# Handing a head pair's row maxima to the score matmuls: a transpose on TensorE against a block transpose on VectorE with the order made by the DRAM loads

## The chip, the cores and the metric

The kernel runs on one core of one Trainium2 chip. The metric is the device time of one execution in microseconds (us). Three executions of the kernel before took 2587.34, 2584.07 and 2585.78 us; the median is 2585.78 us. The engines are named as in the profile: PE is TensorE's matrix unit (PEld is its weight loader), DVE is VectorE, ACT is ScalarE, POOL is GpSimd, SP is SyncE, and SPq or ACTq is the instruction stream of SP or ACT where it issues a DMA (a transfer).

## The reference, cut to what matters

```python
x  = A_x                                   # 1 x 2048 x 576
xn = layernorm(x)
# A: attention with 32 heads of 18, no mask
q, k, v = split(xn @ wqkv)                 # per head 2048 x 18
p  = softmax(q @ k.T * 18 ** -0.5)         # per head 2048 x 2048
s  = concat_heads(p @ v) @ wo
# B: gated feed-forward, 4608 wide
h  = gelu_tanh(xn @ w_gate) * (xn @ w_up)
g  = silu(h @ w_down)
out = x + s * g
```

The softmax subtracts each row's maximum before the exponential. That maximum, one number for each of 2048 queries and each head, is what the change is about.

## The kernel before, in words

**Precision.** The inputs are float32. Before a matmul each operand is split into two float16 numbers, a high and a low part, and the products of the parts are summed.

**Stages.** A short first stage (about 200 us) normalises x, computes the first heads' projections and the row maxima of head pair 0. Then one long loop runs over the 16 head pairs (`for p in range(NPAIR)`, line 1685) with 64 steps each. Everything else, the remaining projections, the feed-forward matmuls (L492 for gate and up, L752 for down) and the output projection, is cut into small pieces and placed between those steps. The order of every engine's instructions is fixed when the program is built: a planner (`make_plan`, `Deferred`, `subtick`) decides with a table of assumed costs which piece follows which, and each engine then works through its own list in that order, waiting on semaphores where it must.

**One step** `i` of pair `p` has these parts:

- The *score pass* (`qk2`, L1395): two matmuls on PE, one per head, make a 128 x 512 block of transposed scores in a buffer `s2`. ACT turns it into exponentials (L1401, or L1403 and L1404 where the two heads need different scales). There is one buffer `s2`, so the next score pass waits until these exponentials are finished.
- The *max pass* (`qk1`, L1343): two matmuls on PE make a block of untransposed scores of pair p+1 (in steps 60 to 63 of pair p+2) in a buffer `s1`. DVE reduces it to row maxima (L1346, `PM`). There is one buffer `s1` as well, so the next max pass waits for that row max.
- Filler pieces on PE, and every few steps a *burst* (L1420) that multiplies the saved exponentials with the values, after which DVE adds the burst's PSUM result to a running sum (L1428, `osb`).

**How the maximum gets into the score pass.** In the score pass the keys' tile KT has 56 rows per head: 54 rows of split keys and two rows holding a constant 2^15. The queries' tile QT has 54 rows of split queries and two rows that hold minus the row maximum times 2^-15, as a high and a low part, for each of 2048 queries. So the matmul subtracts the maximum by itself. But the maxima come out of DVE with the queries on the 128 partitions, and the two rows of QT need the queries along a row. That turn is the handover, made once per pair in three pieces (`max_end`, line 1350), called from the loop for the next pair: `a` at the end of step 59, `b` at the end of step 60, `c` in step 62.

- `a` (DVE): the last reduction `rmx` (L1356) and the high and low parts `rmc` (L1358, L1359), 128 partitions x 64 float16: column = 32 * head + 16 * part + query tile.
- `b`: PE turns `rmc` to 64 x 128 in the PSUM buffer `md_t` (L1365), which bursts and down pieces use too. ACT copies it to SBUF (`rms`, L1367) and stores it in DRAM (`md`, L1369): 64 partitions of 256 bytes.
- `c`: ACT issues two loads, one per head (L1373). Each reads 32 of the 64 DRAM rows, which lie one behind another, as two runs of 4096 bytes, and writes them to the two rows of QT.

The first score pass of the new pair, which is one step after step 63, needs these rows. The handovers are numbered here by the pair that they serve: handover 0 is for pair 0 and lies ahead of the loop (there `b` and `c` stand elsewhere among the pieces), handovers 1 to 15 lie at steps 59 to 62 of pair 0 to 14.

The names in the profile: `s` is the score buffer, `P` the exponentials, `mc` is called `rmc`, `ms` is `rms`. L460 (`touch`) is a tiny DVE read that sets the order of two writers of a PSUM buffer. VT<-VS (L1335) is the load of a pair's values on SP's queue; rd, oc, sd and obr (L1456 to L1471) are small transfers of the softmax sums.

Of the kernel before, what the change touches and what calls it, by code (L numbers as in the profile page):

```python
# [13 lines left out]
F16 = mybir.dt.float16  # L14
I32 = mybir.dt.int32
AF = mybir.ActivationFunctionType
# [4 lines left out]
P = 128  # L21
NT = S // P
# [72 lines left out]
def kernel(ctx: ExitStack, tc: tile.TileContext, x, wqkv, wo, w_gate, w_up, w_down, out):  # L95
    nc = tc.nc
# [4 lines left out]
    sm = ctx.enter_context(tc.tile_pool(name="sm", bufs=3))  # L101
    wp = ctx.enter_context(tc.tile_pool(name="wp", bufs=2))
    ap = ctx.enter_context(tc.tile_pool(name="ap", bufs=2))
    dp = ctx.enter_context(tc.tile_pool(name="dp", bufs=1, space=DRAM))
# [89 lines left out]
    ident = cp.tile([P, P], F16, tag="ident", name="ident")  # L194
# [1123 lines left out]
    QT, KT, VT, PM = {}, {}, {}, {}  # L1318
# [31 lines left out]
    def max_end(p):  # L1350

        st = {}

        def a():
            st["mx"] = sm.tile([P, 2, NT], F32, tag="rmx", name=f"rmx{p}", bufs=2)
            nc.vector.tensor_reduce(st["mx"], PM[p], op=ALU.max, axis=AX.X, negate=True)  # L1356
            st["mc"] = sm.tile([P, 2, 2, NT], F16, tag="rmc", name=f"rmc{p}", bufs=2)
            nc.vector.tensor_scalar(st["mc"][:, :, 0, :], st["mx"], 2.0 ** -15, None, op0=ALU.mult)  # L1358
            nc.vector.scalar_tensor_tensor(  # L1359
                st["mc"][:, :, 1, :], st["mx"], 2.0 ** -15, st["mc"][:, :, 0, :], op0=ALU.mult, op1=ALU.subtract  # L1360
            )

        def b():
            mt = MTile("md", [P, 2048], F16, 0)
            nc.tensor.transpose(mt.t[0:64, 0:P], st["mc"].rearrange("p a b c -> p (a b c)"), ident)  # L1365
            st["ms"] = sm.tile([64, P], F16, tag="rms", name=f"rms{p}", bufs=2)
            nc.scalar.activation(st["ms"], mt.t[0:64, 0:P], AF.Copy)  # L1367
            st["md"] = dp.tile([64, P], F16, tag="md", name=f"md{p}", bufs=2)
            nc.scalar.dma_start(st["md"], st["ms"])  # L1369

        def c():
            for h in range(2):
                nc.scalar.dma_start(  # L1373
                    QT[p][54 + 64 * h:56 + 64 * h, :],
                    st["md"][32 * h:32 * h + 32, :].rearrange("(a t) c -> a (t c)", a=2),
                )
            mdone[p] = 1

        return a, b, c
# [138 lines left out]
    while isinstance(pj1[0], Rest) or pj1[0][0] is None:  # L1518
        f = pj1.pop(0)
# [346 lines left out]
```

## Time and profile before

| | before |
|---|---|
| three runs | 2584.07 to 2587.34 us, median 2585.78 us |
| span of the profiled execution, first to last instruction | 2583.5 us |
| PE busy | 2503.6 us (97%) |
| DVE busy | 1894.5 us (73%) |
| ACT busy | 1660.4 us (64%) |
| POOL busy | 1536.8 us (59%) |
| mean granted TensorE clock | 0.997 |

The profile gives the profiled execution's span, 2583.5 us, and no device time of its own; the median of the three runs is 2.3 us above it, and that is taken as what lies around the span. Times in the views are from the span's start. In a timeline a row reads: start, duration, engine, line, operation, output<-inputs, shapes, how many alike were merged, and in brackets how long the engine had been idle before it and what released it. Matmuls overlap: a pair of 512-column matmuls takes 0.22 us of PE's time, though each is shown with 0.38 to 0.40 us. A row x2 at L1395 or L1343 is one pass (two heads).

### The profile page before, as it was taken

What the parts mean: (1) busy time and instruction counts of PE and PEld (TensorE: products, weight loads), DVE (VectorE), ACT (ScalarE), POOL (GpSimd) and SP (SyncE); (2) the same over time, 40 slices, a digit from 0 to 9 for tenths busy, and PEclk for the clock granted to TensorE, in tenths of its full rate; (3) what the DMA queues carried; (4) which work ended last, traced back from release to release, by engine and by line L of the source; (5) the groups of instructions that cost most, each with busy time, mean ns of one, the idle gap of its engine ahead of it and who ended that gap; (6) DMA issues with size and microseconds to landing.
All of it is one profiled execution on the core that took longest, in us unless ns stands there. A gap on an engine that the chain in (4) does not pass through costs nothing.

```text
span 2583.5 us, 60864 instructions
## 1 busy us (share of the span) xinstructions
PE 2503.6 (97%) x25816; PEld 1316.9 (51%) x25816; DVE 1894.5 (73%) x2595; ACT 1660.4 (64%) x2082; POOL 1536.8 (59%) x1545
## 2 busy tenths in 40 slices
PE   7899999999999999999999999999999999999998
PEld 6554445444544454445445545454544555455555
DVE  7677768777787778777777777776777777777644
ACT  6126666766677666766666666667666666766664
POOL 4346664576357564667576675848576676757513
PEclk9999999999999999999999999999999999999999
DMA  4430121201130112111110111201111111010124
GB/s 154 132 94 21 19 55 43 75 14 29 52 87 16 22 45 63 32 38 47 19 52 16 33 40 29 56 11 37 29 34 29 38 22 45 9 49 12 37 63 139
DMA packets 134635, 118.69 MB, mean 46 GB/s; under 512 B 59691, under 2 KB 113713, under 8 KB 134362
## 3 DMA queue, kind: packets, MB, share of 16 engines
q1 hardware_dynamic: 130089, 106.39, 15.8%
q0 software_dynamic: 1568, 5.37, 0.6%
q8 instruction: 202, 3.31, 0.5%
q10 hardware_dynamic: 2704, 3.03, 0.4%
q14 instruction: 72, 0.58, 0.1%
HBM read 84.89 MB, written 29.61 MB: 44 GB/s over the span
## 4 chain that ended last, share of the span: by engine, by line
PE 82%; DVE 7%; POOL 3%; ACT 3%; issue 2%; DMA 2%; SPq 0%; ACTq 0%; POOLq 0%; DVEq 0%
PE mb_t L492 16%; PE md_t L752 15%; PE ma_t L492 15%; PE md_t L1420 9%; PE s L1395 8%; PE s L1343 8%; PE ma_t L1420 6%; DVE PM L1346 3%; ACT P L1401 1%; PE md_t L931 1%; DVE osb L1428 1%; DMA QT<-QD 1%; POOL raw_c L356 1%; PE pv_t L511 1%; PE mb_t L931 1%
## 5 line engine op out<-in xcount | busy, mean ns | idle before, releaser
L1346 DVE TENSOR_REDUCE PM<-s 128x2 f32<-128x1024 f32 x1024 | 1251.0, 1224 | 335.5 <-PE s L1343 327.6
L1401 ACT ACTIVATE P<-s,etab 128x1024 f32<-128x1024 f32 x896 | 995.6, 1112 | 590.2 <-PE s L1395 579.4
L492 PE MATMUL ma_t<-XHT,whi_c 64*128 64x512 f16 x1440 | 542.0, 376 | 4.3 <-DVE osb L1428 2.2
L492 PE MATMUL mb_t<-XHT,whi_c 64*128 64x512 f16 x1440 | 541.7, 376 | 2.3 <-DVE touch L460 1.5
L492 PE MATMUL ma_t<-XHT,wlo_c 64*128 64x512 f16 x1296 | 487.4, 376 | 0.0
L492 PE MATMUL ma_t<-XL,whi_c 64*128 64x512 f16 x1152 | 433.2, 376 | 0.0
L492 PE MATMUL mb_t<-XHT,wlo_c 64*128 64x512 f16 x1152 | 433.2, 376 | 0.0
L492 PE MATMUL mb_t<-XL,whi_c 64*128 64x512 f16 x1152 | 433.0, 376 | 0.0
L1395 PE MATMUL s<-QT,KT 56*128 56x512 f16 x2048 | 404.4, 380 | 6.6 <-ACT P L1401 2.6
L1343 PE MATMUL s<-KT,QT 54*128 54x512 f16 x2048 | 398.3, 378 | 12.0 <-DVE PM L1346 9.7
L492 PEld LDWEIGHTS <-whi_c 64*128 64x128 f16 x5184 | 273.9, 94 | 241.0 <-issue 19.3
L752 PE MATMUL md_t<-dhi_c,hhi 64*128 64x288 f16 x2304 | 341.3, 283 | 4.8 <-DVE touch L460 2.1
L752 PE MATMUL md_t<-dhi_c,hlo 64*128 64x288 f16 x2304 | 341.0, 282 | 0.0
L752 PE MATMUL md_t<-dlo_c,hhi 64*128 64x288 f16 x2304 | 340.5, 282 | 0.0
L752 PEld LDWEIGHTS <-hhi 64*128 64x128 f16 x4608 | 246.7, 94 | 140.4 <-issue 16.8
L715 POOL TENSOR_TENSOR hlo<-gv,hhi 128x512 f16<-128x512 f32 x144 | 167.3, 1162 | 215.0 <-ACT hhi L708 210.7
L693 POOL TENSOR_SCALAR tw<-tw 128x512 f32<-128x512 f32 x144 | 90.7, 630 | 341.2 <-ACT tw L686 340.9
L1420 PE MATMUL md_t<-P,VT 128*32 128x512 f32 x2472 | 291.9, 596 | 0.5 <-ACT P L1401 0.5
L1395 PEld LDWEIGHTS <-KT 56*128 56x128 f16 x2048 | 123.5, 94 | 244.2 <-issue 156.4
L680 POOL TENSOR_TENSOR tw<-gs 128x512 f32<-128x512 f32 x144 | 151.0, 1049 | 125.2 <-ACT gs L657 125.1
L772 DVE SCALAR_TENSOR_TENSOR y<-md_t,c_c,y 128x576 f32<-128x576 f32 x272 | 219.5, 807 | 8.2 <-PE md_t L752 8.2
L492 PEld LDWEIGHTS <-wlo_c 64*128 64x128 f16 x2592 | 138.0, 94 | 118.9
(270 smaller groups left out, 4061.5 us busy)
## 6 DMA issues: line engine op xcount, KB each, us to landing
draw_c<-in_B_w_down SPq DMA_DIRECT2D x18, 576.0 KB
raw_c<-in_B_w_gate SPq DMA_DIRECT2D x18, 512.0 KB
raw_c<-in_B_w_up SPq DMA_DIRECT2D x18, 512.0 KB
obr<-rd SPq DMA_DIRECT2D x30, 256.0 KB
KT<-KD SPq DMA_DIRECT2D x32, 224.0 KB
QT<-QD SPq DMA_DIRECT2D x32, 216.0 KB
VS<-vst POOLq DMA_DIRECT2D x16, 304.0 KB, 2.6
VT<-VS SPq DMA_DIRECT2D x16, 304.0 KB
```

The lines of the kernel that those rows point to most:

```text
L492: nc.tensor.matmul(o, lw, xx, start=self.stage == 0 and self.k == 0, stop=self.stage == 1 and self.k == self.slots - 1, skip_group_check=True,
L680: gp.tensor_tensor(st["t"], st["g"], st["g"], op=ALU.mult)
L693: gp.tensor_scalar(st["t"], st["t"], 1.0, 1.0, op0=ALU.mult, op1=ALU.add)
L715: gp.tensor_tensor(hs.lo[:, ft], st["v"], hs.hi[:, ft], op=ALU.subtract)
L752: nc.tensor.matmul(self.t.t[:, hf, 0:288], a[r, ft, sl], b[r, ft, 288 * hf:288 * hf + 288], start=self.stage == 0 and k == 0, stop=self.st ...
L772: nc.vector.scalar_tensor_tensor(yy, y, w.c, yy, op0=ALU.mult, op1=ALU.add)
L931: nc.tensor.matmul(o, a, b, start=self.stage == 0 and self.k == 0, stop=self.stage == 1 and self.k == len(terms) - 1, skip_group_check=True,)
L1343: nc.tensor.matmul(s1[:, h], QT[p][r, P * qt:P * qt + P], KT[p][r, 512 * kb:512 * kb + 512], start=True, stop=True)
L1346: nc.vector.tensor_reduce(PM[p][:, :, qt, kb:kb + 1], s1, op=ALU.max, axis=AX.X)
L1395: nc.tensor.matmul(s2[:, h], KT[p][r, P * kt:P * kt + P], QT[p][r, 512 * qb:512 * qb + 512], start=True, stop=True)
L1401: nc.scalar.activation(pt, s2, AF.Exp, scale=ETAB[j0])
L1420: nc.tensor.matmul(t.t[qd:qd + 32, :], VT[p][:, c0:c0 + 32], pt[:, h], start=kt == k0, stop=kt == k1, skip_group_check=True,)
```

## The change

`b` no longer uses PE, PSUM or an ACT copy. DVE transposes `rmc` in blocks of 32 x 32 to a tile `mt` (still named `rms`) of 128 partitions x 64, and ACT stores that to DRAM as 128 rows of 128 bytes. After the block transpose, row 32 * b + 16 * part + tile of `mt` holds at column 32 * head + j the value for query 128 * tile + 32 * b + j. So a head's row of QT lies in DRAM in 64 pieces of 32 values (64 bytes), and `c`'s two loads pick these up in order by their access pattern. `a` and the places of `a`, `b` and `c` in the loop are as before.

```diff
         def b():
-            mt = MTile("md", [P, 2048], F16, 0)
-            nc.tensor.transpose(mt.t[0:64, 0:P], st["mc"].rearrange("p a b c -> p (a b c)"), ident)
-            st["ms"] = sm.tile([64, P], F16, tag="rms", name=f"rms{p}", bufs=2)
-            nc.scalar.activation(st["ms"], mt.t[0:64, 0:P], AF.Copy)
-            st["md"] = dp.tile([64, P], F16, tag="md", name=f"md{p}", bufs=2)
-            nc.scalar.dma_start(st["md"], st["ms"])
+            st["mt"] = sm.tile([P, 64], F16, tag="rms", name=f"rms{p}", bufs=2)
+            nc.vector.transpose(st["mt"], st["mc"].rearrange("p a b c -> p (a b c)"))
+            st["md"] = dp.tile([P, 64], F16, tag="md", name=f"md{p}", bufs=2)
+            nc.scalar.dma_start(st["md"], st["mt"])
 
         def c():
+            md = st["md"]
             for h in range(2):
                 nc.scalar.dma_start(
-                    QT[p][54 + 64 * h:56 + 64 * h, :],
-                    st["md"][32 * h:32 * h + 32, :].rearrange("(a t) c -> a (t c)", a=2),
+                    QT[p][54 + 64 * h:56 + 64 * h, :].rearrange("a (t b j) -> a t b j", t=NT, b=4),
+                    bass.AP(
+                        tensor=md.tensor, offset=md.offset + 32 * h,
+                        ap=[[NT * 64, 2], [64, NT], [2 * NT * 64, 4], [1, 32]],
+                    ),
                 )
             mdone[p] = 1
```

The rest of the program keeps its order on all engines; only the numbers in names differ, and lines below the change are numbered two higher. Three places show what moves, all at handover 9.

On DVE, before: `s_9_63` is the last max pass for pair 9, `s_10_0` and `s_10_1` are the max passes of steps 60 and 61.

```order
L1346 TENSOR_REDUCE PM_19121<-s_9_63_21563 128x2
L1428 TENSOR_TENSOR osb_1_20724<-md_t,osb_1_20724 128x512
L1356 TENSOR_REDUCE rmx_21589<-PM_19121 128x32
L1358 TENSOR_SCALAR rmc_21591<-rmx_21589 128x2x16
L1359 SCALAR_TENSOR_TENSOR rmc_21591<-rmx_21589,rmc_21591 128x2x16
L1346 TENSOR_REDUCE PM_21302<-s_10_0_21599 128x2
L1346 TENSOR_REDUCE PM_21302<-s_10_1_21633 128x2
```

And with the change:

```order
L1356 TENSOR_REDUCE rmx_21571<-PM_19105 128x32
L1358 TENSOR_SCALAR rmc_21573<-rmx_21571 128x2x16
L1359 SCALAR_TENSOR_TENSOR rmc_21573<-rmx_21571,rmc_21573 128x2x16
L1346 TENSOR_REDUCE PM_21284<-s_10_0_21581 128x2
L1365 STREAM_TRANSPOSE rms_21604<-rmc_21573 128x64
L1346 TENSOR_REDUCE PM_21284<-s_10_1_21613 128x2
```

The new transpose stands behind the row max of step 60, not right behind `rmc`, because `b` is recorded at the end of step 60. In handovers 1, 4 and 12 the sum of a burst (`osb`) stands ahead of it as well, in handover 11 a reduction of weights (L262); in handovers 0 and 15 it follows `rmc` directly.

On ACT, before (`P_2_14` to `P_3_15` are the exponentials of steps 60 to 63 of pair 8, `P_0_0` the first of pair 9):

```order
L1401 ACTIVATE P_2_14_21597<-s_8_2_14_21594,etab_5383 128x1024
L1367 ACTIVATE rms_21624<-md_t 64x128
L1369 DMA md_21626<-rms_21624 64x128
L1401 ACTIVATE P_3_14_21631<-s_8_3_14_21628,etab_5383 128x1024
L1401 ACTIVATE P_2_15_21661<-s_8_2_15_21658,etab_5383 128x1024
L1373 DMA QT_19115<-md_21626 2x2048 x2
L686 ACTIVATE tw_0_1_21603<-tw_0_1_21603 128x512
L1401 ACTIVATE P_3_15_21707<-s_8_3_15_21704,etab_5383 128x1024
```

And with the change:

```order
L1403 ACTIVATE P_2_14_21579<-s_8_2_14_21576,etab_5379 128x1024
L1367 DMA md_21606<-rms_21604 128x64
L1403 ACTIVATE P_3_14_21611<-s_8_3_14_21608,etab_5379 128x1024
L1403 ACTIVATE P_2_15_21641<-s_8_2_15_21638,etab_5379 128x1024
L1372 DMA QT_19099<-md_21606 2x64x32 x2
L686 ACTIVATE tw_0_1_21585<-tw_0_1_21585 128x512
L1403 ACTIVATE P_3_15_21687<-s_8_3_15_21684,etab_5379 128x1024
```

The store stays where it was, between the exponentials of steps 60 and 61; the copy ahead of it is gone.

On PE, before:

```order
L492 MATMUL mb_t<-XHT,wlo_c_19573 128x512
L1365 LDWEIGHTS rmc_21591
L1365 MATMUL md_t<-ident,rmc_21591 64x128
L1395 LDWEIGHTS KT_16878
L1395 MATMUL s_8_3_14_21628<-QT_16877,KT_16878 128x512
L1395 LDWEIGHTS KT_16878
L1395 MATMUL s_8_3_14_21628<-QT_16877,KT_16878 128x512
L1343 LDWEIGHTS QT_21296
L1343 MATMUL s_10_1_21633<-KT_21297,QT_21296 128x512
```

With the change the two L1365 rows are not there, and the score pass of step 61 follows the filler directly:

```order
L492 MATMUL mb_t<-XHT,wlo_c_19555 128x512
L1397 LDWEIGHTS KT_16864
L1397 MATMUL s_8_3_14_21608<-QT_16863,KT_16864 128x512
L1397 LDWEIGHTS KT_16864
L1397 MATMUL s_8_3_14_21608<-QT_16863,KT_16864 128x512
L1343 LDWEIGHTS QT_21278
L1343 MATMUL s_10_1_21613<-KT_21279,QT_21278 128x512
```

So PE loses its wait for `rmc` ahead of the score pass of step 61, and its max pass of step 61 comes next as before.

## The prediction

> **What bounds the kernel now.** I read the page first, then the groups by line of PE. One row of each kind:
>
> ```profile
> span 2583.5 us, 60864 instructions
> L1343 PE MATMUL s<-KT,QT 54*128 54x512 f16 x2048 | 398.3, 378 | 12.0 <-DVE PM L1346 9.7 <-DMA QT<-QD 0.9 <-DVE touch L460 0.2
> L1365 PE MATMUL md_t<-ident,rmc 128*64 128x128 f16 x16 | 3.8, 238 | 4.4 <-DVE osb L1428 2.4 <-DVE rmc L1359 1.9
> L1365 PEld LDWEIGHTS <-rmc 128*64 128x64 f16 x16 | 1.7, 106 | 10.3 <-DVE rmc L1359 6.1 <-issue 1.7 <-DVE PM L1346 1.7
> ```
>
> PE is the full engine (97% in the table ahead), so whatever delays PE for good is time. The sixteen turns (L1365) look costly: PE idles 4.4 us before them, its weight loader 10.3 us, mostly for DVE. But the max pass L1343 also waits for DVE's row max, 9.7 us in all, so I followed the single handovers in the timeline, on PE, DVE and ACT together. Handover 9, the common kind:
>
> ```profile
> 1530.27 1.22 DVE L1346 TENSOR_REDUCE PM<-s 128x2 f32<-128x1024 f32 x1
> 1530.40 0.24 PE L1365 MATMUL md_t<-ident,rmc 128*64 128x128 f16 x1 [0.17 <-DVE rmc L1359]
> 1530.58 0.39 PE L1395 MATMUL s<-QT,KT 56*128 56x512 f16 x2
> 1530.98 0.46 ACTq L1369 DMA_DIRECT2D md<-rms  x1
> 1531.49 1.11 ACT L1401 ACTIVATE P<-s,etab 128x1024 f32<-128x1024 f32 x1 [0.54 <-PE s L1395]
> 1531.54 0.39 PE L1343 MATMUL s<-KT,QT 54*128 54x512 f16 x2 [0.57 <-DVE PM L1346]
> 1531.97 1.23 DVE L1346 TENSOR_REDUCE PM<-s 128x2 f32<-128x1024 f32 x1 [0.48 <-PE s L1343]
> 1533.13 0.40 PE L1395 MATMUL s<-QT,KT 56*128 56x512 f16 x2
> 1533.57 1.11 ACT L1401 ACTIVATE P<-s,etab 128x1024 f32<-128x1024 f32 x1 [0.96 <-PE s L1395]
> ```
>
> The reader is to see that PE turns, makes its score pass (step 61), and then stands 0.57 us at the max pass until the row max of step 60 ends (1530.27 + 1.22 = 1531.49). DVE, not PE, sets the time of that max pass. A PE that reaches it earlier waits longer.
>
> **The change part by part.** *PE's turn goes.* In ten handovers (2, 3, 5 to 10, 13, 14) the max pass behind the turn waits for the row max as in handover 9; there the removal alone gives nothing. In the others it can give something, below.
>
> *DVE gets a transpose.* For its duration I take the line through a DVE operation on 32 columns, 0.19 us (L1359), and the block transposes that the kernel has already, on 512:
>
> ```profile
> 2432.81 0.19 DVE L1359 SCALAR_TENSOR_TENSOR rmc<-rmx,rmc 128x32 f16<-128x32 f32 x1
> L1443 DVE STREAM_TRANSPOSE obr<-osb 128x512 f32<-128x512 f32 x2 | 1.4, 712 | 0.1
> L1358 DVE TENSOR_SCALAR rmc<-rmx 128x32 f16<-128x32 f32 x16 | 6.5, 408 | 0.6
> L1467 SPq DMA_DIRECT2D rd<-oc x30: 319/336/417, 296.0 to 2454.9; - x30
> ```
>
> (0.712 - 0.19) / 480 = 1.09 ns a column, so 64 columns take 0.22 us. Lower bound 0.19. Upper bound: L1358 has 32 columns too and yet a mean of 0.41 us, so some small DVE operations are stretched; if the transpose is one of those it takes 0.4 us and more. I take 0.22. It stands between two row maxima, where DVE idles 0.48 us (1531.97): covered. Were that cover gone it would cost 0.22 x 16 = 3.5 us.
>
> *The store now waits for DVE.* It is still ahead of the exponentials of step 61 on ACT, but the transpose it waits for stands behind the row max of step 60. From the end of that row max: transpose 0.22, release 0.05 (as from 1531.49 to 1531.54), issue 0.34 (L1467 also moves 128 pieces of 64 bytes), next ACT instruction 0.05 (1530.98 + 0.46 to 1531.49): 0.66 us. In handover 9 the exponentials start at 1531.49 + 0.66 = 1532.15 instead of 1531.49, end 1.11 later, and release the next score pass at 1533.31 instead of 1533.13: **0.18 us lost**, because a new wait takes the place of the old one. Handover 14 is the other end of the ten:
>
> ```profile
> 2284.53 1.22 DVE L1346 TENSOR_REDUCE PM<-s 128x2 f32<-128x1024 f32 x1
> 2287.61 0.39 PE L1395 MATMUL s<-QT,KT 56*128 56x512 f16 x2 [0.24 <-ACT P L1401]
> ```
>
> 2285.75 + 0.66 + 1.11 + 0.05 = 2287.57, level with 2287.61: there ACT's copy and store were in the way already. Five of the ten (3, 5, 8, 9, 10) read like handover 9, two lose about 0.05, three (2, 7, 14) nothing: 5 x 0.18 + 0.1 = **1.0 us lost**. Bounds: 0.5 with a 0.19 us transpose and a shorter issue, 4 with 0.41 us and a longer one.
>
> *Handovers behind a burst (1, 4, 12).* The turn shares `md_t` with the burst and waits for DVE to add its result. Handover 12, then handover 15, where the transpose follows `rmc` directly, then 11:
>
> ```profile
> 1981.79 0.69 DVE L1428 TENSOR_TENSOR osb<-md_t,osb 128x512 f32<-128x512 f32 x1 [0.75 <-PE md_t L1420]
> 1982.53 0.22 PE L1365 MATMUL md_t<-ident,rmc 128*64 128x128 f16 x1 [0.81 <-DVE osb L1428]
> 1983.60 1.12 ACT L1401 ACTIVATE P<-s,etab 128x1024 f32<-128x1024 f32 x1 [0.54 <-PE s L1343]
> 1984.76 0.39 PE L1395 MATMUL s<-QT,KT 56*128 56x512 f16 x2
> 2433.35 0.24 PE L1365 MATMUL md_t<-ident,rmc 128*64 128x128 f16 x1
> 2434.45 1.11 ACT L1401 ACTIVATE P<-s,etab 128x1024 f32<-128x1024 f32 x1 [0.54 <-PE s L1395]
> 2435.61 0.39 PE L1395 MATMUL s<-QT,KT 56*128 56x512 f16 x2
> 1832.00 0.67 DVE L262 TENSOR_REDUCE m_c<-raw_c 128x1 f32<-128x512 f32 x1
> 1833.09 0.69 ACT L1403 ACTIVATE P<-s,etab 128x512 f32<-128x512 f32 x1 [0.54 <-PE s L1343]
> ```
>
> In 12 PE could go on about 1.0 us sooner (0.81 of wait, and the turn), but the transpose stands behind `osb` too: 1982.48 + 0.66 = 1983.14 for the exponentials instead of 1983.60. PE gains 0.46, in handover 1 as much: **0.9 gained**. In 15 `rmc` is ready at 2432.81 + 0.19 = 2433.00 and the store is out by 2433.00 + 0.22 + 0.05 + 0.34 = 2433.61, so the exponentials wait for PE alone: the score pass takes the turn's place at 2433.35, exponentials 0.44 later (1533.13 to 1533.57), 2433.79 instead of 2434.45: **0.65 gained**. In 11 the transpose stands behind a weight reduction that ends at 1832.67: 1832.67 + 0.66 = 1833.33 instead of 1833.09, **0.25 lost**.
>
> *The loads.* Before, a head's two rows are two runs of 4096 bytes; now 128 pieces of 64 bytes. What that costs is not in the trace; the nearest rows are two other transfers (issue, then windows with PE, PEld, DVE, ACT, POOL, clock, share of the 16 DMA engines, GB/s), and the tightest handover, 13:
>
> ```profile
> 1514.10 0.56 SPq L1335 DMA_DIRECT2D VT<-VS  x1
> 1515.00:1515.40 0.40, 0.40 (x6) 0.19 (x4) 0.40 (x1) 0.40 (x1) 0.40 (x1) 1.00 0.00 0
> 1515.60:1516.90 1.30, 1.30 (x18) 0.80 (x16) 0.79 (x2) 0.68 (x2) 1.30 (x2) 1.00 1.17 200
> 585.00:587.00 2.00, 2.00 (x22) 0.93 (x20) 1.78 (x3) 0.80 (x2) 0.00 (x0) 1.00 0.26 99
> 1176.80:1177.10 0.30, 0.30 (x6) 0.16 (x4) 0.30 (x1) 0.30 (x1) 0.30 (x1) 1.00 0.28 28
> 2139.36 0.54 ACTq L1373 DMA_DIRECT2D QT<-md  x2
> 2142.54 0.40 PE L1395 MATMUL s<-QT,KT 56*128 56x512 f16 x2
> ```
>
> VT<-VS moves 2048 pieces of 152 bytes in rows of 16; it is issued in 0.56 us, moves nothing for 1.3 us, then all 16 engines at 200 GB/s: 12.5 GB/s an engine, 12 ns a piece. The window at 585 is obr<-rd, whose source has 4 rows: share 0.26, four engines. So I expect two engines for a source and target with 2 rows at the outside, 64 pieces each: issue 0.56 each, data from 1.3 us on, 64 x 12 ns = 0.8 us. First head 2.1 us after the first issue, second 2.7 (own engines) to 2.9 (the same two). Handover 13 leaves 2142.54 - 2139.36 = 3.18 us: hidden, barely. The upper bound is oc<-sd, 128 pieces of 64 bytes on 16 engines within 0.3 us: up to 37 ns a piece, 128 x 37 ns + 1.3 = 6 us. I stay near 12 ns, since that is a long stream and the other is mostly start. The Trainium skill (DMA: Bandwidth & Descriptors, section "Why a DMA increments its semaphore by 16 and not by 1") says that a transfer runs on the largest number of engines up to 16 that divides the slowest dimension of both sides, and on the lowest-numbered ones: by it both loads share two engines and the second lands at 2.9 us.
>
> Handover 4 is short of that already, since its store meets VT<-VS:
>
> ```profile
> 786.74 0.54 ACTq L1373 DMA_DIRECT2D QT<-md  x2
> 787.33 0.69 ACT L1403 ACTIVATE P<-s,etab 128x512 f32<-128x512 f32 x1 [1.25 <-DMA QT<-md]
> 788.64 0.39 PE L1395 MATMUL s<-QT,KT 56*128 56x512 f16 x2 [1.04 <-ACT P L1404]
> ```
>
> ACT stands at the loads until the store has landed, and PE waits for ACT. Two issues of 0.56 instead of 0.54 together put the exponentials 0.6 us later, and the second head's rows land at 786.74 + 2.9 = 789.64, 1.0 us after the pass that needs them: **1.0 lost** (0.3 if the store lands 0.5 us earlier and the heads don't share engines; 1.5 if a piece takes 16 ns).
>
> *Handover 0* runs while the first weights load:
>
> ```profile
> 185.60 0.24 PE L1365 MATMUL md_t<-ident,rmc 128*64 128x128 f16 x1 [0.87 <-DVE rmc L1359]
> 190.50:194.90 4.40, 4.38 (x41) 2.05 (x39) 1.23 (x2) 0.00 (x0) 3.94 (x5) 1.00 0.77 221
> ```
>
> PE gains up to 1.2 us at the turn (0.87, the turn and its neighbours), and the loads, at 64 pieces an engine among transfers that hold 77% of the engines, may come up to 3 us late. I take zero.
>
> Sum: gained 0.9 + 0.65 = 1.55; lost 1.0 + 0.25 + 1.0 = 2.25. The profiled execution becomes 2583.5 + 0.7 = 2584.2; with the 2.3 us by which the runs' median of 2585.8 lies above the span, **2586.5 us**: no change that can be measured. A measurement of this kernel tells about 0.2%, 5.2 us, from no change.
>
> **The rivals.** *The whole turn comes out (faster).* PE gets its own 16 x 0.18 us (1530.40 to 1530.58) and between 4.4 and 10.3 us of wait: 7.3 to 13.2, about 10 us, 2576 us. For it: PE is the engine that is full. Against it: behind ten of the turns stands a wait for the same DVE, and the store's new place. It needs the store not to hold ACT.
>
> *The loads come late (slower).* One mechanism, at the first score pass of each new pair: 64-byte pieces on two engines. It decides from 3.2 us after the issue, that is from about 15 ns a piece; at 25 ns, half way to the upper bound, the second head lands at 1.3 + 128 x 0.025 = 4.5 us, and handover 13 loses 1.3 us. Eleven of fifteen handovers leave under 4 us between those two rows, about 1 us lost each: 11 us, **2597 us**. For it: the pieces are small and few engines carry them. Against it: VT<-VS at 12 ns.
>
> *The transpose is stretched (slower).* Like L1358, 0.41 us: each of the ten loses 0.19 more, and so does the burst's gain: 2.5 us, 2589 us; to pass 5.2 us it would have to take twice that. Against it: the transposes of L1443 show 0.71 both times. The Trainium skill (SBUF — State Buffer, section "Who interferes with whom") says that a DVE instruction with one SBUF input outside the two-port modes doesn't contend with GpSimd, and doesn't count transposes among those that enter them; no run here shows it.
>
> **How the numbers follow.** No change 0.66, the whole turn 0.12, late loads 0.18, stretched beyond 5.2 us 0.04. The forecast's own range, from the bounds above (gains 1 to 3, losses 1 to 6), is 2584 to 2591. For 8 in 10 I reach into both sides, to 2580 and 2595. Faster by over 0.2%: 0.12, within: 0.66, slower: 0.22.
>
> **What would show it.** In the changed profile: a transpose of about 0.22 us; PE's wait for row maxima at L1343 up from 9.7 us by about 2 us; the exponentials of step 61 in handover 9's kind 0.6 us after the row max's end; PE's next score pass there released by ACT; loads that take over 0.5 us each to issue, and no wait of PE for QT<-md outside handovers 0 and 4. If PE waits for QT<-md in many handovers, the late loads are right; if the exponentials of step 61 start as early as before, the transpose came sooner than I place it.

## The result, and the profile after

| | before | changed |
|---|---|---|
| median, us | 2585.8 (2582.4 to 2588.0, 11 runs) | 2590.5 (2587.9 to 2594.5, 11 runs) |
| ratio to before | | 1.0021, 95% interval 1.0013 to 1.0029 |
| profiled execution's span, us | 2583.5 | 2588.3 |

The changed kernel is slower by about 5 us. PE is busy for 2503.6 us in either profile, though it makes sixteen matmuls fewer. First the page and the groups of the changed kernel, with its transpose and its loads, the queue of ACT (packets, MB, share), and below them the score pass as the profile of before has it:

```profile
span 2588.3 us, 60933 instructions
L1343 PE MATMUL s<-KT,QT 54*128 54x512 f16 x2048 | 400.4, 378 | 16.7 <-DVE PM L1346 14.0 <-DMA QT<-QD 1.3 <-DVE touch L460 0.2
L1397 PE MATMUL s<-QT,KT 56*128 56x512 f16 x2048 | 406.8, 380 | 12.3 <-DMA QT<-md 5.4 <-ACT P L1406 3.5 <-ACT P L1403 2.9
L1365 DVE STREAM_TRANSPOSE rms<-rmc x16: 227/235/246, 184.7 to 2438.9; 128x64 f16<-128x64 f16 x16
L1372 ACTq DMA_DIRECT2D QT<-md x32: 592/628/1257, 188.8 to 2442.0; - x32
q10 hardware_dynamic: 7760, 3.03, 0.4%
...
L1395 PE MATMUL s<-QT,KT 56*128 56x512 f16 x2048 | 404.4, 380 | 6.6 <-ACT P L1401 2.6 <-ACT P L1404 2.0 <-DVE PM L1346 1.3
```

The turns' waits (4.4 us on PE) are gone and the max pass has them in their place: its wait for row maxima is 14.0 us, it was 9.7. The transpose takes 0.235 us and at most 0.246. New is the wait of the score pass for `QT<-md`, 5.4 us. It is two waits, and both are in handover 0.

Handover 9, the common kind, in the changed kernel's timeline:

```profile
1535.65 1.22 DVE L1346 TENSOR_REDUCE PM<-s 128x2 f32<-128x1024 f32 x1
1536.79 0.23 DVE L1365 STREAM_TRANSPOSE rms<-rmc 128x64 f16<-128x64 f16 x1
1536.92 0.39 PE L1343 MATMUL s<-KT,QT 54*128 54x512 f16 x2 [1.09 <-DVE PM L1346]
1537.05 0.32 ACTq L1367 DMA_DIRECT2D md<-rms  x1
1537.48 1.11 ACT L1403 ACTIVATE P<-s,etab 128x1024 f32<-128x1024 f32 x1 [2.16 <-PE s L1343]
1538.64 0.39 PE L1397 MATMUL s<-QT,KT 56*128 56x512 f16 x2
1539.21 1.26 ACTq L1372 DMA_DIRECT2D QT<-md  x2
```

The row max ends at 1536.87, the exponentials of step 61 start 0.61 us later, and the next score pass starts 1.77 us behind the row max; before it was 1.64. The new chain costs 0.12 or 0.13 us, as the step "the store now waits for DVE" has it (0.18). The last row is the two loads. By the trace's packets their 256 pieces move from 1540.63 to 1541.94, all there 2.7 us after the first issue, with 11 ns a piece; they start in pairs, as on two engines.

Handover 0 is where the time goes. First PE's first score pass of pair 0 before the change; then the changed kernel's issue of the loads, that score pass, and windows (PE, PEld, DVE, ACT, POOL, granted clock, DMA share, GB/s):

```profile
198.32 0.39 PE L1395 MATMUL s<-QT,KT 56*128 56x512 f16 x2 [1.32 <-DVE PM L1346]
...
188.84 7.29 ACTq L1372 DMA_DIRECT2D QT<-md  x2
197.45 0.39 PE L1397 MATMUL s<-QT,KT 56*128 56x512 f16 x1 [2.39 <-DMA QT<-md]
200.81 0.58 PE L1397 MATMUL s<-QT,KT 56*128 56x512 f16 x1 [2.98 <-DMA QT<-md]
198.00:200.00 2.00, 0.00 (x0) 0.00 (x0) 0.00 (x0) 0.81 (x1) 0.00 (x0) 0.91 0.25 75
200.00:202.00 2.00, 1.19 (x6) 0.48 (x7) 0.14 (x1) 0.57 (x1) 0.00 (x0) 0.50 0.24 64
202.00:204.00 2.00, 2.00 (x12) 0.88 (x10) 1.67 (x2) 1.06 (x2) 0.76 (x2) 0.50 0.00 0
204.00:206.00 2.00, 2.00 (x12) 0.81 (x10) 0.30 (x1) 0.73 (x1) 1.92 (x2) 0.50 0.00 0
```

PE stands 2.39 us for the first head and 2.98 for the second. Counted from `rmx`, the first head's matmul starts at 13.5 us, as before the change; the second head's starts at 16.9 us, where before both started at 13.5. And when it has both, its clock is at half: 12 matmuls in 2 us where before had 20. The records of the granted clock put it at 0.50 from 199.63 to 206.46, twice 3.41 us.

Handover 4 in the same way (the store, the loads, the exponentials behind them, the score pass, two windows):

```profile
785.50 0.32 ACTq L1367 DMA_DIRECT2D md<-rms  x1
789.61 1.26 ACTq L1372 DMA_DIRECT2D QT<-md  x2
790.98 0.69 ACT L1405 ACTIVATE P<-s,etab 128x512 f32<-128x512 f32 x1 [2.04 <-DMA QT<-md]
792.30 0.65 PE L1397 MATMUL s<-QT,KT 56*128 56x512 f16 x2 [1.83 <-ACT P L1406]
793.00:794.00 1.00, 1.00 (x10) 0.50 (x8) 0.79 (x1) 0.95 (x1) 0.92 (x2) 0.77 0.00 0
794.00:795.00 1.00, 1.00 (x6) 0.35 (x4) 0.43 (x1) 0.16 (x1) 0.82 (x1) 0.50 0.00 0
```

ACT stands at the loads until the store has landed, PE waits 1.83 us for ACT where it waited 1.04, and 1.3 us later the clock halves here too, for 3.41 us.

What each handover took, changed minus before, from the start of `rmx` (L1356) to that of the new pair's fifth score pass, in the two profiles (negative is gained):

| handover | predicted | measured | | handover | predicted | measured |
|---|---|---|---|---|---|---|
| 0 | 0 | **+5.6** | | 8 | +0.18 | +0.06 |
| 1 | -0.46 | -0.54 | | 9 | +0.18 | +0.12 |
| 2 | 0 | +0.02 | | 10 | +0.18 | +0.15 |
| 3 | +0.18 | +0.18 | | 11 | +0.25 | +0.17 |
| 4 | +1.0 | **+2.3** | | 12 | -0.46 | -0.30 |
| 5 | +0.18 | +0.12 | | 13 | +0.05 | 0.00 |
| 6 | +0.05 | +0.02 | | 14 | 0 | +0.13 |
| 7 | 0 | -0.09 | | 15 | -0.65 | -0.70 |

The sum is +7.2. Between the handovers the profile of before stands 2.3 us longer, in places that differ from one profile to the next; the spans differ by 4.9.

### The profile page after: what moved, and what is told of

It is laid out like the page before. It is cut to its first block, busy times and chain, and to the rows that moved or that the text cites. A ratio compares the mean times of both kernels' runs of the same rounds, so it can differ in the third digit from the quotient of the medians.

```text
span 2588.3 us, 60933 instructions
## 1 busy us (share of the span) xinstructions
PE 2503.6 (97%) x25800; PEld 1313.7 (51%) x25800; DVE 1895.2 (73%) x2611; ACT 1659.1 (64%) x2066; POOL 1539.7 (59%) x1545
## 4 chain that ended last, share of the span: by engine, by line
PE 81%; DVE 7%; POOL 3%; DMA 3%; ACT 2%; issue 2%; SPq 0%; ACTq 0%; POOLq 0%; DVEq 0%
PE md_t L752 15%; PE mb_t L492 15%; PE ma_t L492 15%; PE md_t L1422 9%; PE s L1397 8%; PE s L1343 8%; PE ma_t L1422 6%; DVE PM L1346 3%; ACT P L1403 1%; PE md_t L931 1%; DMA QT<-QD 1%; DVE osb L1430 1%; POOL raw_c L356 1%; PE mb_t L931 1%; PE pv_t L511 1%
```

## Experiments

Each ratio is to the kernel before, timed beside it on the same chip (medians of before 2585.2 to 2586.0 us), with its 95% interval.

### Where the time goes: handover 0 alone, or all but it

The edit of `h0_old`; `h0_new` has the two branches exchanged:

```diff
         def b():
+            if p == 0:
+                (PE's turn, ACT's copy and the store as before)
+            else:
                 (VectorE's transpose and the store as changed)
         def c():
+                if p == 0:
+                    (the two contiguous loads as before)
+                    continue
```

> Handover 0 alone keeps PE's turn, the old store and the two loads of 4096-byte runs; the other fifteen are as in the changed kernel. Theory (the loss sits in handover 0: its loads land late, PE stands, and the granted clock falls to 0.50 for 6.8 us behind it): 2590.5 - 5.5 = 2585.0 us, no wait of PE for QT<-md, granted clock 1.00 from 195 to 210 us. Rival (the loss is spread over the fifteen handovers of the loop, and the offset at handover 0 is drift): above 2589.5 us.

> The kernel before, with handover 0 alone done the new way (VectorE transpose, permuting loads). Theory: 2585.8 + 5.5 = 2591.3 us, with the clock at 0.50 for 3.4 or 6.8 us behind handover 0. Rival (spread): below 2587 us.

`h0_old`: 2586.5 us, 1.0003 (0.9994 to 1.0012). Handover 0 costs 0.0 in its profile. `h0_new`: 2592.1 us, 1.0028 (1.0017 to 1.0039), handover 0 costs 5.0 there and the clock is at 0.50 for 6.8 us behind it. So one handover of sixteen carries the loss: 4 us come back when it is undone, 7 are lost when it alone is done. `h0_old` stands 1.5 us higher than expected; in its profile handover 4 costs 4.1 us, with the clock at half for 6.8 us (below).

### What makes the loads late

The first idea was the order of issues: head 1's load comes out of ACT at 195.5 only, behind eight stores `OHL<-zeros` that SP issues from 192.7 on. `zero_late` moves these:

```diff
-    zero_last()
     pend = []
...
+            if i == 8 and p == 0:
+                zero_last()
             if i == 52 and p + 2 < NPAIR:
```

> The changed kernel, with the eight OHL<-zeros stores (L826) moved from ahead of the loop to step 8 of pair 0, so that SP issues nothing behind draw_c while handover 0's loads are out. Theory (head 1's load is issued at 195.5 us behind SP's zero stores, which run from 192.7 to 201, and its pieces wait for them): head 1 lands near 197.5 in place of 200.3 us, PE's second wait for QT<-md (2.98 us) is under 0.5, the clock stays 1.00 or falls for one period of 3.4 us only, and the time is 2586 to 2587.5 us. Rival (the pieces wait for the weight loads on their own engines, which were issued before): nothing moves, 2590.5 us.

It measured 2590.1 us, 1.0019 (1.0010 to 1.0028): nothing moved, and that theory fell. ACT is indeed no longer held, and yet the second head's matmul starts as late. Its issue, its PE row, and the packets of the DMA view from 196.6 to 201.0 (q1 is SP's queue, with the weights; q10 ACT's):

```profile
190.49 1.83 ACTq L1372 DMA_DIRECT2D QT<-md  x2
201.82 0.58 PE L1397 MATMUL s<-QT,KT 56*128 56x512 f16 x1 [2.31 <-DMA QT<-md]
q1 hardware_dynamic: 160, 0.20, 12.4%
q10 hardware_dynamic: 151, 0.01, 2.4%
```

12.4% of sixteen engines is two engines, and they are full with weights: 160 packets, nearly all of 1024 or 2304 bytes, against 151 of ours. In the trace the packets alternate one for one, 11 ns for a piece of 64 bytes and 46 ns for 1024 bytes of weights. All 256 pieces take from 195.16 to 201.35 us: 6.19 us / 128 = 48 ns a piece on either engine, against some 10 in handover 9. The Trainium skill (DMA: Bandwidth & Descriptors, section "Queues, rings and completion order") says that an engine goes round the queues that have work for it packet by packet; the trace agrees that the two queues take turns, with one piece of 64 bytes and one packet of weights at a time, where that section calls 9 to 17 descriptors in a packet typical.

In the changed kernel itself the second head is late in another way. By its trace's packets, head 0's 128 pieces move from 193.57 to 196.86 us, 51 ns a piece on either engine. Head 1's move from 199.75 to 200.29 us, 0.55 us for as many: they are quick, but their issue came only at 195.53, and the first of them moved 4.2 us behind it. So the second head is as late with the issue held (16.9 us behind `rmx`) as with the issue free and its pieces slow (`zero_late`, 16.4 us). In both kernels the first data come 4.7 us behind the first issue, against 1.4 in handover 9. That was so before the change too (4.5 us), but the four runs of 4096 bytes were then all there 0.6 us later.

Would more engines help? `rows4` splits each load by its row, so that the slowest dimension is 16 tiles in place of 2 rows:

```diff
             for h in range(2):
+                for a in range(2):
                     nc.scalar.dma_start(
-                        QT[p][54 + 64 * h:56 + 64 * h, :] ...   (2, 16, 4, 32)
+                        QT[p][r:r + 1, :] ...                   (1, 16, 4, 32), r = 54 + 64 * h + a
```

> The changed kernel with four loads, one for each row of QT, in place of two; the same 256 pieces of 64 bytes, but the slowest dimension is now 16 tiles, so that 16 engines carry them, 4 pieces each. Theory (in handover 0 the pieces stand in line on two engines behind weight loads): head 0 and head 1 both land within 2.5 us of their issue in the loop, PE's wait for QT<-md in handover 0 falls from 5.4 us to under 2, the clock doesn't fall there, and the time is 2586 to 2587 us, with up to 1.2 us more in handover 4 for two more issues on ACT. Rival (the issue on ACT is what is held up while the weights load, whatever the engines): four issues are held as long as two, 2590 us or more.

It measured 2604.2 us, 1.0073 (1.0059 to 1.0087), the slowest of all. Four issues cost more than the engines could save. Handover 9 of `rows4`, and its wait by source:

```profile
1548.47 3.33 ACTq L1374 DMA_DIRECT2D QT<-md  x4
1553.53 0.39 PE L1399 MATMUL s<-QT,KT 56*128 56x512 f16 x2 [1.02 <-ACT P L1405]
PEld L1399 <- DMA QT<-md: 12.6, 11, 2.6
```

ACT is held for 3.33 us in place of 1.26, the last row lands 4.3 us after the first issue, and both the exponentials and the rows of QT are late: handovers 2, 3, 5, 7 to 10, 13 and 14 lose 0.6 to 1.3 us each. In handover 0 ACT is held for 12.5 us and 7.2 are lost. This is the rival of the late loads as the prediction described it, set off by issues instead of slow pieces. On how many engines these pieces ran the trace doesn't tell.

`big_loads` puts the pieces on the store's side, so that the loads are runs of 4096 bytes as before:

```diff
-            nc.scalar.dma_start(st["md"], st["mt"])
+            for h in range(2):
+                nc.scalar.dma_start(
+                    bass.AP(tensor=md.tensor, offset=md.offset + 32 * P * h, ap=[[32, 4], [P, 32], [1, 32]]),
+                    st["mt"][:, 32 * h:32 * h + 32],
+                )
```

> VectorE's transpose stays, but the order is put right by the store (two stores, one for each head, 128 pieces of 64 bytes each) and the two loads are again runs of 4096 bytes. Theory (handover 0 loses by the form of its loads): its loads are issued within 1.1 us and land before PE needs them, 4.5 us back; the second store holds ACT 0.3 us longer ahead of the exponentials of step 61, 0.3 us lost in each of some eight handovers, 2.4 us; together 2588.5 us. Rival (the loads are late because the weights load then, whatever their form): 2590.5 + 2.4 = 2593 us.

2596.5 us, 1.0044 (1.0031 to 1.0057): a miss on the price, not on the direction. Handover 0 costs 1.7 us in place of 5.6. But the second store is dear everywhere else. Handover 9 of `big_loads`:

```profile
1538.26 1.09 ACTq L1369 DMA_DIRECT2D md<-rms  x2
1540.62 0.39 PE L1402 MATMUL s<-QT,KT 56*128 56x512 f16 x2 [0.71 <-ACT P L1408]
```

One issue of 128 pieces into a permuted target takes 0.53 us where the plain one took 0.32, and there are two. The exponentials of step 61 come 0.76 us later than in the changed kernel, and eleven handovers lose 0.7 to 1.0 us each, 9.3 together; I had put 0.3 on each of some eight.

`sp_first` leaves the loads as changed, and takes the weights out of their way in handover 0:

```diff
-                nc.scalar.dma_start(
+                (nc.scalar if p else nc.sync).dma_start(
                     QT[p][54 + 64 * h:56 + 64 * h, :].rearrange("a (t b j) -> a t b j", t=NT, b=4),
...
-            lead=8 if i == 3 else 1, ...
+            lead=14 if i == 3 else 1, ...
```

> The changed kernel, with handover 0's two loads (the same 256 pieces of 64 bytes) issued on SP's queue ahead of the weight loads raw_c and draw_c, in place of on ACT's queue beside them; the weights follow on the same queue, some 4 us later, and the background work on them is ordered a little later. Theory (the pieces are slow among the weight loads: 48 ns a piece on two engines there, 10 ns alone): the loads land within 3 us of the first issue, as in the loop, PE doesn't wait for QT<-md at handover 0, the clock stays 1.00 there, 2590.5 - 5.5 = 2585.0 us. Rival (the form of the loads is slow at this place whatever is beside it): PE waits over 2 us for QT<-md, 2589 us or more.

2585.5 us, 1.0003 (0.9994 to 1.0012), as the theory had it (2585.0). Handover 0 of `sp_first`, the loads on SP and the first score pass:

```profile
189.10 1.38 SPq L1372 DMA_DIRECT2D QT<-md  x2
197.13 0.39 PE L1397 MATMUL s<-QT,KT 56*128 56x512 f16 x2 [1.32 <-DVE PM L1346]
```

PE waits only for the row max, as it did before the change, and the clock stays at 1.00. Handover 0 now gains 1.2 us, the turn's price. By the trace's packets the 256 pieces move from 190.60 to 191.92 us, 1.3 us as in handover 9. So the same pieces cost nothing ahead of the weight loads and some 5 us among them. The edit also takes SP's queue in place of ACT's and orders the background work a little later; but in handover 9 the pieces are as quick on ACT's queue, so the queue alone is not the cause. How much of the lateness belongs to the held issue and how much to slow pieces stays open.

### Standing, or the clock

PE stands about 3 us longer at handover 0 than before, and loses 5.6. Three kernels fill the standing with matmuls that nobody reads: if the standing is what makes the clock fall, it should then stay at 1.00. `h0_fill` writes them into the score tile itself:

```diff
         for h in range(2):
             r = slice(64 * h, 64 * h + 56)
+            for _ in range((9, 11)[h] if (p, qb, kt) == (0, 0, 0) else 0):
+                f = slice(64 * h, 64 * h + 54)
+                nc.tensor.matmul(s2[:, h], KT[p][f, 0:P], QT[p][f, 0:512], start=True, stop=True)
```

> The changed kernel, with 9 and 11 matmuls that compute nothing of use put ahead of the two matmuls of pair 0's first score pass (some 2.0 and 2.4 us of PE work, inside the 2.4 and 3.0 us that PE stands there; the real matmuls overwrite their result). Theory (of the 5.5 us about half is the standing itself, the other half the clock at 0.50 that follows): the real matmuls start as late as before, the granted clock stays 1.00 from 198 to 207 us, 2590.5 - 2.8 = 2587.7 us. Rival (all of it is the standing): 2590.5 us or more, since the work is more.

2588.6 us, 1.0016 (1.0007 to 1.0025), but its profile shows the clock at 0.50 from 198.4 on all the same; its score tile had to wait 1.31 us for a row max first. `fill2` therefore writes `md_t`, which is free there:

```diff
+        ft = MTile("md", [P, 512], F32, 0).t if idle[0] else None
...
+            for _ in range(idle[h]):
+                nc.tensor.matmul(ft, KT[p][0:54, 0:P], QT[p][0:54, 0:512], start=True, stop=True)
```

> As h0_fill, but the 9 and 11 useless matmuls of handover 0 write the md_t tile, which is free there, so that they start as soon as PE stands and don't wait for a row max. Theory (half of handover 0's loss is the clock): the granted clock stays 1.00 from 195 to 207 us, the two real matmuls start at 197.5 and 200.8 us as in the changed kernel, and the time is 2590.5 - 2.8 = 2587.7 us. Rival (it is all standing): 2590.5 us.

2590.0 us, 1.0015 (1.0006 to 1.0024): no better, and inconclusive on the question. Its windows show that the clock fell although PE was busy:

```profile
200.00:202.00 2.00, 2.00 (x9) 0.83 (x9) 0.00 (x0) 0.86 (x1) 0.00 (x0) 0.76 0.24 73
202.00:204.00 2.00, 2.00 (x10) 0.82 (x8) 0.07 (x1) 0.50 (x1) 0.00 (x0) 0.50 0.25 66
```

Its fillers use 54 of the 128 rows of the array, one at a time, while the kernel's own matmuls at this place run in pairs, on rows 0 to 63 and 64 to 127 at once. So `fill3` pairs them:

```diff
+        ft = MTile("md", [P, 2, 512], F32, 0).t if idle[0] else None
...
+            for k in range(2 * idle[h]):
+                f = slice(64 * (k % 2), 64 * (k % 2) + 54)
+                nc.tensor.matmul(ft[:, k % 2], KT[p][f, 0:P], QT[p][f, 0:512], start=True, stop=True)
```

> As fill2, but each useless matmul has a twin on the other row group (rows 0 to 53 and 64 to 117, as in a real score pass), so that 9 and 11 pairs use twice as much of the array in the same time. Theory (the clock falls behind a window of 3.41 us in which too little of the array is in use, and half of handover 0's loss is that): the granted clock stays 1.00 from 195 to 207 us, the two real matmuls start at 197.5 and 200.8 us as in the changed kernel, 2590.5 - 2.8 = 2587.7 us. Rival (the clock follows something else, or the loss is all standing): 2590 us or more.

2587.1 us, 1.0013 (1.0004 to 1.0022). The windows of `fill3`, with the second head's matmul:

```profile
201.20 0.37 PE L1402 MATMUL s<-QT,KT 56*128 56x512 f16 x1 [0.63 <-DMA QT<-md]
198.00:200.00 2.00, 2.00 (x22) 0.91 (x20) 0.00 (x0) 1.05 (x1) 0.00 (x0) 1.00 0.19 64
200.00:202.00 2.00, 1.37 (x13) 0.52 (x11) 0.17 (x1) 0.39 (x1) 0.00 (x0) 1.00 0.29 75
202.00:204.00 2.00, 2.00 (x22) 1.00 (x18) 1.87 (x3) 1.68 (x3) 0.62 (x1) 1.00 0.03 9
```

The real matmul starts as late as ever (201.20), the clock stays at 1.00, and handover 0 costs 3.1 us in place of 5.6. So about 3 us of it is standing and 2.5 the clock. The other profiles agree: handover 0 costs 4.3 us where the clock halves for one period (`early`, below) and 5.0 to 5.8 in the five profiles where it halves for two. The mean granted clock over eleven runs is 0.9973 for `fill3` and 0.9957 for `fill2` and the changed kernel. Forty useless matmuls make the kernel faster in the median by 3.4 us; but the ratio's interval overlaps those of the changed kernel and of `fill2`, so the share of the clock rests on the profiles.

### Handover 4, and the rest

`h04_old` is `h0_old` with `p in (0, 4)` for `p == 0`.

> Handovers 0 and 4 keep PE's turn, the old store and the old loads; the other fourteen are as in the changed kernel. Theory (handover 4 costs some 1 us of waiting and 1.5 to 3 us of halved clock behind it, and nothing else is lost in sum): 2586.5 - 3 = 2583.5 us, granted clock 1.00 at 790 to 800 us. Rival (handover 4 costs 1.0 us, as predicted): 2585.5 us.

2582.6 us, 0.9991 (0.9983 to 1.0000). Against `h0_old`, 1.3 us over before, that is 4.3 us for handover 4 alone by the medians and 3.1 by the ratios, and no halved clock is left in its profile near 790. In the profiles handover 4 costs 0.9 and 1.4 us where the clock holds (`h0_fill`, `fill3`), 2.3 to 3.3 with one period at half (the changed kernel, `fill2`, `zero_late`, `sp_first`) and 4.1 with two (`h0_old`); done the old way it still differs from before by 0.2 (`h04_old`) and 0.4 (`h0_new`). That the other fourteen handovers together gain is not shown: in this profile they sum to -0.3 us, and the interval of the ratio reaches 1.0000.

`early` moves the transpose up to stand directly behind `rmc`, ahead of the row max of step 60:

```diff
         def a():
             ...                                   (rmx, rmc)
+            st["mt"] = sm.tile([P, 64], F16, tag="rms", ...)
+            nc.vector.transpose(st["mt"], ...)
         def b():
-            st["mt"] = sm.tile([P, 64], F16, tag="rms", ...)
-            nc.vector.transpose(st["mt"], ...)
```

> The changed kernel, with the transpose directly behind rmc (step 59) in place of behind the row max of step 60; the store and the loads stay where they are. Theory (the 0.12 us lost in handovers 3, 5, 8, 9, 10 and the 0.17 in 11 come from the store's wait for the transpose, behind the row max): the exponentials of step 61 wait for PE alone, these six come back with a little of the turn, some 1.0 us, and the store of handover 4 is issued a us sooner; handover 0 stays as it is: 2588 to 2589.5 us. Rival (these losses come from DVE's extra work itself): 2590.5 us.

2586.9 us, 1.0004 (0.9995 to 1.0013): better than expected, and for another reason. The common handovers get worse, 0.26 us lost in place of 0.12. Handover 9 of `early`:

```profile
1532.07 0.24 DVE L1364 STREAM_TRANSPOSE rms<-rmc 128x64 f16<-128x64 f16 x1
1532.24 1.19 DVE L1346 TENSOR_REDUCE PM<-s 128x2 f32<-128x1024 f32 x1
1533.48 0.39 PE L1343 MATMUL s<-KT,QT 54*128 54x512 f16 x2 [1.35 <-DVE PM L1346]
```

The row max that everyone waits for now stands behind the transpose: DVE's cover is gone, and its 0.24 us are paid. That part of my expectation was wrong. The gain comes from the bursts, where the transpose no longer waits for `osb`: handovers 1 and 12 gain 1.0 and 1.1 us. The largest part is handover 4. There the store is out at 782.06, ahead of `VT<-VS` at 783.84, so that ACT's stand at the loads (2.04 us in the changed kernel) shrinks:

```profile
782.06 0.32 ACTq L1368 DMA_DIRECT2D md<-rms  x1
783.84 0.57 SPq L1335 DMA_DIRECT2D VT<-VS  x1
787.44 0.69 ACT L1406 ACTIVATE P<-s,etab 128x512 f32<-128x512 f32 x1 [0.55 <-DMA QT<-md]
```

Handover 4 gains 1.25 us there in place of losing 2.3. Handover 0 costs 4.3 in this profile in place of 5.6, since its clock halves for one period in place of two; this edit doesn't touch handover 0, so that part of the profile's gain is not its doing.

### Each handover by its best way

`mix` takes the old way in handovers 0, 3, 5, 8, 9 and 10, the early transpose in 1, 4, 11, 12 and 15, and the change as it is in 2, 6, 7, 13 and 14:

```diff
+            if p in (1, 4, 11, 12, 15):
+                turn()                            (in a: VectorE's transpose, behind rmc)
         def b():
+            if p in (0, 3, 5, 8, 9, 10):
+                (PE's turn, copy and store)       (and in c the contiguous loads)
+            else:
+                if p not in (1, 4, 11, 12, 15):
+                    turn()
```

> Handovers 0, 3, 5, 8, 9 and 10 the old way (PE's turn), handovers 1, 4, 11, 12 and 15 with VectorE's transpose directly behind rmc, handovers 2, 6, 7, 13 and 14 as in the changed kernel. Theory (each handover's gain or loss is its own, and they add up): against the kernel before 0 in the first six, -1.0 -1.3 0.0 -1.1 -0.7 in the five, -0.1 in the rest: 2585.9 - 4.2 = 2581.7 us. Rival (the offsets of single handovers are swallowed by the next stage's waits): 2585 to 2586 us.

2580.3 us, 0.9979 (0.9970 to 0.9987): faster than both kernels. Measured as in the table above, the six old handovers change by 0.02 us at most, handovers 1, 4, 12 and 15 by -1.0, -1.1, -1.1 and -0.7, and nothing is given back behind them; the rival of swallowed offsets falls. The time is 1.4 us better than the theory's 2581.7 us, and where that comes from no run here shows.

## Why the prediction was right or wrong

**Near in time, wrong on its dearest place.** 2586.5 us were predicted, 2590.5 measured, inside the range and inside the forecast's own. The likeliest case said no change by over 0.2%; it came out at 0.21%, with an interval (0.13 to 0.29%) that lies on both sides of that bound.

**The turn that goes: right.** The turns' 4.4 us of waits are gone, and the max pass waits 4.3 us longer for row maxima, 3.3 of it in the handovers; the prediction's sign said about 2. Handover 9 got nothing for its turn. The rival of the whole turn is refuted by that row.

**The transpose: right.** 0.235 us against 0.22, and it was never stretched (227 to 246 ns), though `rmc` beside it kept its mean of 0.41 us. That it is covered holds only behind the row max: `early` took the cover away and paid it in full.

**The store's wait: right, a third too dear.** 0.61 us from the row max to the exponentials against 0.66, so 0.12 us a handover in place of 0.18. The transpose started 0.08 us ahead of the row max's end (1536.79 against 1536.87) and the issue took 0.32 in place of 0.34, while the way from the issue to the exponentials took 0.11 in place of 0.05. Handovers 1, 12, 15 and 11 came within 0.2 us of their terms. Together these fourteen were put at -0.3 and measured at -0.7.

**The loads in the loop: right.** Two engines, 11 ns a piece, data from 1.4 us on, all there at 2.7 us; handover 13 hidden to the hundredth. The late loads are refuted in the loop and came true in one place. (Their price rested on eleven handovers with under 4 us between the first issue and the score pass; before the change there are ten.)

**Handover 0: the term that failed.** "The loads ... may come up to 3 us late. I take zero." The bound was near: PE stood some 3 us longer, all of it for the second head. The choice of zero was not worked out from anything. The row for it was quoted, with 77% of the DMA engines busy, while the 12 ns of a piece and the 1.3 us to the first data came from a stretch in which one transfer had the engines to itself. Among the weights a piece costs 48 to 51 ns, more than the 37 ns that were the upper bound, and the first data come 4.7 us behind the issue. With these two the step's own sum gives 4.7 + 128 x 0.048 = 10.8 us behind the first issue (10.9 measured in `zero_late`), where handover 0 had left 7.85 before the change (190.47 to 198.32). In the changed kernel the second issue was held on top, which the prediction had no term for; the last piece landed 11.45 us behind the first issue. The 1.2 us that PE could gain at the turn, which the prediction named and dropped, are what `sp_first` gains. What had no term at all is the clock: a stall of PE has a second price behind it, 2.5 us here.

**Handover 4: mechanism right, the same term missing.** Where the clock held it cost 0.9 and 1.4 us (`h0_fill`, `fill3`) against 1.0. In the changed kernel's profile the loads were issued 0.5 us sooner behind `rmx` than before (8.4 against 8.9 us), and the score pass came 0.30 us later, as the bound for an earlier store had it (0.3); the rest of the 2.3 us came with the halved clock. Between the medians of `h0_old` and `h04_old` it was 4.3.

## What to carry to other kernels

A price for a DMA piece, and for the time to its first data, holds only for the company in which it was measured: here the loads with two rows at the outside ran on two engines, and among the weights' packets on these engines each small piece waited for one of them. A stall of PE of nearly 2 us should be given a second term for the clock that may fall behind it. And where one edit is repeated at many places, its sum has terms of both signs; taking it only where its own row gains can turn a loss into a gain.

## What the hardware showed that was not expected

**The clock falls by windows, and seemingly by how much of the array is used.** The spells at 0.50 last 3.41 us or a multiple of it, save the last of each profile, which the end cuts, and within an execution they begin a whole number of 3.41 us apart. In fourteen profiles, between 150 and 2490 us, seventeen such windows were followed by a halved clock. Counting rows times columns times length of the matmuls started in them, against an array that is full all the time (512 columns in 0.21 us), these windows had at most 0.37 of the array in use. Of the more than 9500 others, outside the halved spells, three to eighteen had as little, depending on how the float32 matmuls are counted; since a few matmul records are missing, some may be miscounted. PE's busy share separates them less well: `fill2` halved behind a window that was 72% busy (0.29 of the array), while one that was 48% busy (0.42 of the array, also in `fill2`) kept the clock. Neither measure is clean: one window of `h0_fill`, 47% busy with 0.36 of the array, kept it too. `fill2` against `fill3` is the one trial of it, so this is a reading and not settled. The Trainium skill (TensorE: Matmul & The Clock Gate, section "What's actually happening") has the window of 3413 ns, free-running, and a halved clock behind an idle one. The trace agrees on the length; but here 1.83 us of standing in handover 4 were enough, in a window that was 46% busy.

Where a stall falls in these windows differs from one execution to the next, and with it the price: in handover 4 PE stands 1.83 us in the changed kernel and the clock halves for one period, 2.52 in `h0_old` for two, and 2.63 in `fill3` for none. Not every halving is the change's: at 908 to 914 us, where no handover lies, `h0_new`, `zero_late` and `sp_first` show one too. The mean granted clock over the runs follows the times: 0.9973 for 23 runs of before, 0.9957 for the changed kernel, 0.9974 for `h0_old`, 0.9980 for `h04_old`. From before to changed that is 0.0016 x 2590 = 4.1 us of full clock not granted, an upper bound for what the clock took of the 5 us.

**A DMA issue can hold its engine.** In handover 0 the two issues kept ACT from 188.84 to 196.13 us (7.29 us; 1.26 in the loop), while SP issued the weights and the zeros. Without the zeros behind them (`zero_late`) they took 1.83. What the issue waited for no run here shows.
